# The last mantissa bits on GpSimd, and the product with v ahead of the sinks' transposes

## The chip, the cores and the metric

The program runs on one core of a Trainium2 chip. That core has five engines, each with an instruction queue of its own that is worked off in order: TensorE (PE in the profile, its weight loads PEld), VectorE (DVE), ScalarE (ACT), GpSimd (POOL) and SyncE (SP), which here only issues DMA transfers. The metric is the device time of one execution in microseconds (us), from repeated runs; one further execution is recorded by the profiler.

## The reference, cut to what matters

Attention over 2 batches, 8 heads, 768 positions and head size 64. A query sees the first 4 positions (the sinks) and a window of 128 positions behind it. A feed-forward layer (512 to 2048 and back) and a mixing layer over channels and positions follow.

```
keep = is_sink | in_window
scores = np.where(keep, scale * q @ k.T, -1e9)
a = softmax(scores);  x = a @ v
x = x + relu(layernorm(x) * g_ln @ w_ch1) @ w_ch2
theta = x @ w_theta
u = x + w_tok_r @ (x * cos(theta)) + w_tok_i @ (x * sin(theta))
out = u + relu(u @ w_ch)
```

## The kernel before, in words

**Pieces.** The 2 x 768 positions are cut into six pieces of 256 (two tiles of 128); pieces 0 to 2 are batch 0, pieces 3 to 5 batch 1. `attn_fast` walks the 48 steps (piece, head). In a step PE computes the scores of both tiles (L274 and L275, or L278), DVE adds the mask and takes the maximum (L381), and ACT the exponential (L384). One step later `turn_w` has PE transpose the window's weights into a PSUM bank (L397), and ACT and DVE copy them out as two 16-bit parts (L400, L401).

**Sinks.** The first tile of a batch sees the sinks inside its own window, so pieces 0 and 3 (those that begin a batch) have no sinks apart. The other four do: their weights for the first 16 positions are transposed on their own by `turn_sinks` (two transposes, L410) into columns 256 to 511 of a bank, from which ACT (L411) and DVE (L412) copy them into one of three `ws` buffers. That is 4 pieces x 8 heads = 32 times.

**The product with v.** One step after that, `values` multiplies the transposed weights with v (L426) into columns 0 to 127 of a bank called `pv`, and `normalize` (L441, DVE) scales the result into x. `finish` takes one `pv` bank for two things that belong to two different steps: the sinks' transposes of the step just turned, and the product with v of the step before it. The product reads the `ws` that was written one step earlier.

**Order.** PE's order is written out by hand: the generator of the attention yields between its parts, and `run` fills in the feed-forward layer's products (`first` L605 and L625, `second` L651) from the moment the first piece is normalised. With one piece in the feed-forward layer its products are half as wide as with two. The order on ACT, DVE, POOL and SP is set by the compiler's scheduler. Three to seven PSUM banks are handed round (`bank`).

**Weights.** They arrive as 64-bit floats. `load64` puts together a 32-bit float from one: DVE masks the sign and the top (L502), ACT scales the high word (L503), ACT takes the last mantissa bits from the low word (L505, a 16-bit read with step 4 and a 16-bit write with step 2), and DVE joins the parts (L506). It runs for 32 tiles of 128x512 (feed-forward weights, within the first 90 us) and 20 more later (theta 4, tok 12 of 128x768, ch 4). SP issues the loads (L498) into a few staging buffers, which L506 frees. Each weight is then split into two parts, by ACT (L593, L668) and POOL (L594, L669). POOL also splits q and k (L234, L249), scales and splits v (L204, L205) and adds up x in the gate (L722).

Of the kernel before, what the change touches and what calls it, by code (L numbers as in the profile page):

```python
# [14 lines left out]
AF = mybir.ActivationFunctionType  # L15
ALU = mybir.AluOpType
# [55 lines left out]
class Net:  # L72
# [207 lines left out]
    def attn_fast(self, eng):  # L280

        steps = [(piece, h) for piece in range(NP) for h in range(H)]
        nc, p, qk, pending, turned, late = self.nc, self.att, {}, [], [], []

        def load(j, eng=eng):
            if j < len(steps):
                piece, h = steps[j]
                if piece >= STACKED:
                    qk[piece, h] = self.stack_qk(piece, h, nc.gpsimd)
                elif h % 2 == 0:  # L290
                    qk[piece, h] = qk[piece, h + 1] = self.split_qk(piece, h // 2, eng)

        def load_v(piece):
            if piece < NP:
                b, tiles = self.tiles(piece)
                for t in tiles + ([NT] if tiles[-1] >= 2 else []):
                    self.split_v(b, t)

        def first_of_all(piece):
            return self.ahead() if piece == 0 else ExitStack()  # L300

        def turn():

            piece, h, pt, st = pending.pop(0)
            b, tiles = self.tiles(piece)
            with first_of_all(piece):
                wt, blocks = self.turn_w(pt, tiles)
            p["ws"].append(p["ws"].pop(0))
            turned.append((piece, h, wt, p["ws"][-1], blocks, st))
            return (pt, p["ws"][-1]) if tiles[0] else None  # L310

        def finish(sinks, ready):

            bank = self.bank("pv")
            if sinks:
                self.turn_sinks(bank, *sinks)
            if not ready:
                return
            piece, h, wt, ws, blocks, st = turned.pop(0)
            b, tiles = self.tiles(piece)  # L320
            with first_of_all(piece):
                self.values(bank, b, h, tiles, piece, wt, ws, blocks, st)
                if h % (H // 2) == H // 2 - 1:
                    self.stats(piece, h // (H // 2))
            if h == V_RANGE:
                while late:
                    q, ts = self.tiles(late.pop())
                    for t in ts:
                        with self.behind():
                            self.range_v(q, t)  # L330
            if h == H - 1:
                with first_of_all(piece):
                    self.norm(piece)
                late.append(piece)

        load(0, self.nc.vector)
        load_v(0)
        for j, (piece, h) in enumerate(steps + [(NP, 0)] * (TURN + LAG)):
            if j < len(steps):
                b, tiles = self.tiles(piece)  # L340
                if h == 0:
                    self.x[piece] = self.xp.tile([128, PIECE, DM], F32, tag=f"x{piece}", name=f"x{piece}")
                if piece < STACKED:
                    load(j + 2)
                if piece >= STACKED or h == H - 1 and piece + 1 == STACKED:
                    load(j + 1)
                if h == (3 if piece else V_NEXT):
                    load_v(piece + 1)
                pt, st = yield from self.softmax(h, tiles, qk[piece, h])
                pending.append((piece, h, pt, st))  # L350
            sinks = None
            if len(pending) > (TURN if j < len(steps) else 0):
                sinks = turn()
                yield
            ready = len(turned) > (LAG if j < len(steps) + TURN else 0)
            if sinks or ready:
                finish(sinks, ready)
                yield
        for t in tiles:
            self.range_v(b, t)  # L360
# [51 lines left out]
        nc.vector.scalar_tensor_tensor(out=ws[32:32 + NSK], in0=ps, scalar=PSC, in1=ws[0:NSK], op0=ALU.mult,  # L412
                                       op1=ALU.subtract)

    def values(self, pv, b, h, tiles, piece, wt, ws, blocks, st):

        nc = self.nc
        hc = slice(h * D, (h + 1) * D)
        for i in range(len(tiles)):
            prods = [(wt[:, x + e * len(blocks)], v[:, hc]) for e in range(2) for x, (j, t) in enumerate(blocks) if j == i  # L420
                     for v in self.v3[b, t][:2 - e]]
            if tiles[0]:
                vk = self.v3[b, NT]
                prods += [(ws[0:32 + NSK, i], vk[0:32 + NSK, 0, hc]), (ws[0:NSK, i], vk[0:NSK, 1, hc])]
            for j, (a, m) in enumerate(prods):
                nc.tensor.matmul(pv[:, i * D:(i + 1) * D], a, m, start=j == 0, stop=j == len(prods) - 1)  # L426
        self.normalize(h, pv, st, self.x[piece])

    def tiles(self, piece):
# [63 lines left out]
    def load64(self, src, stage, dst, tag):  # L493

        nc = self.nc
        n = dst.shape[-1]
        raw = stage.tile([128, n, 2], I32, tag=tag, name="raw")
        nc.sync.dma_start(out=raw.rearrange("p n w -> p (n w)"), in_=src.bitcast(I32))  # L498
        hi, flat = raw[:, :, 1], raw.rearrange("p n w -> p (n w)")
        half = flat.bitcast(U16).rearrange("p (n w) -> p n w", w=4)  # L500
        parts = dst.bitcast(U16).rearrange("p (n w) -> p n w", w=2)
        nc.vector.tensor_scalar(out=parts[:, :, 1], in0=half[:, :, 3], scalar1=0x8000, scalar2=None, op0=ALU.bitwise_and)  # L502
        nc.scalar.activation(hi.bitcast(F32), hi.bitcast(F32), AF.Copy, scale=2.0 ** -112)  # L503

        nc.scalar.activation(parts[:, :, 0], half[:, :, 1], AF.Copy, scale=2.0 ** -13, bias=2.0 ** -14 - 0.5)  # L505
        nc.vector.scalar_tensor_tensor(out=dst, in0=hi, scalar=3, in1=dst, op0=ALU.logical_shift_left,  # L506
                                       op1=ALU.bitwise_or)

# [537 lines left out]
```

## Time and profile before

| | |
|---|---|
| median of 3 runs | 755.43 us (754.74 to 755.86) |
| the profiled execution's own time | 753.02 us |
| its span | 751.2 us |
| PE busy | 650.8 us (87%) |
| DVE busy | 367.9 us (49%) |
| ACT busy | 365.6 us (49%) |
| POOL busy | 273.8 us (36%) |
| mean granted TensorE clock | 0.928 |

The span is the time from the first to the last instruction; 1.8 us of the profiled execution lie around it. Busy is the time in which an engine had at least one instruction running. [...]

### The profile page before, as it was taken

Reading aid. Unit: us, or ns where it says so; the run is one execution under the profiler, and the core shown is the slowest. Engines: PE = TensorE matmul, PEld = TensorE weight load, DVE = VectorE, ACT = ScalarE, POOL = GpSimd, SP = SyncE. Lnnn points to the kernel's source line nnn. Section 1 sums busy time; section 2 is a strip of 40 time slices with the busy share of each in tenths; the row PEclk is TensorE's granted clock in tenths of the full one; section 3 lists DMA queues with packets and bytes.
Section 4 is the critical chain, followed back from the end, with each engine's and each line's share of the span. In section 5 each row is a group of like instructions: output and inputs, shape, how many; then the busy total and the mean of one; then the engine's idle time right before and its main releaser. Section 6 shows DMA issues by size and latency. Waiting matters only on the chain.

```text
span 751.2 us, 10135 instructions
## 1 busy us (share of the span) xinstructions
PE 650.8 (87%) x3747; PEld 523.7 (70%) x3747; DVE 367.9 (49%) x808; ACT 365.6 (49%) x774; POOL 273.8 (36%) x240
## 2 busy tenths in 40 slices
PE   3845898789889997889888889999989989899996
PEld 2633556666667675666656667778878988899996
DVE  5889624432335434353333434321367878874442
ACT  5798724344445563444434425643456656552220
POOL 3143102422437585444354117654402343330000
PEclk9999758778999998989989969999999999999999
DMA  6587401100211131110110011310011232200102
GB/s 242 185 312 262 176 20 32 30 16 0 60 31 52 44 97 40 37 38 19 37 38 1 0 57 60 123 43 0 1 31 55 85 127 71 85 15 29 37 15 82
DMA packets 19339, 50.38 MB, mean 67 GB/s; under 512 B 2769, under 2 KB 5841, under 8 KB 19281
## 3 DMA queue, kind: packets, MB, share of 16 engines
q1 hardware_dynamic: 19280, 49.66, 19.8%
q8 instruction: 31, 0.51, 0.3%
q14 instruction: 28, 0.22, 0.1%
HBM read 46.50 MB, written 3.15 MB: 66 GB/s over the span
## 4 chain that ended last, share of the span: by engine, by line
PE 38%; DVE 6%; ACT 3%; issue 1%; POOL 1%; DMA 1%; ACTq 0%; POOLq 0%; DVEq 0%
PE m L736 11%; PE h L625 8%; PE acc L651 7%; PE f L767 4%; PE th L695 4%; PE pv L426 1%; DVE st L506 1%; DVE hl L630 1%; DVE st L502 1%; DMA raw<-wtok 1%; PE tp L680 1%; DVE k L705 1%; ACT hh L629 0%; PE s L275 0%; DMA raw<-wth 0%
## 5 line engine op out<-in xcount | busy, mean ns | idle before, releaser
L594 POOL TENSOR_TENSOR wl<-w,wh 128x512 fp32r<-128x512 f32 x92 | 119.6, 1304 | 176.2 <-ACT wh L593 105.4
L625 PE MATMUL h<-xT,wh 128*128 128x512 f32 (+1 forms) x408 | 115.1, 419 | 7.6 <-DVE hl L630 7.6
L593 ACT ACTIVATE wh<-w 128x512 fp32r<-128x512 f32 x102 | 63.9, 628 | 111.0 <-PE acc L651 66.3
L625 PEld LDWEIGHTS h<-xT,wh 128*128 128x128 f32 x408 | 75.0, 210 | 27.0 <-DVE hl L630 11.2
L426 PE MATMUL pv<-v,wt 128*128 128x64 f16 x528 | 33.3, 206 | 64.9 <-DVE ws L412 55.7
L381 DVE CUSTOM_DVE_ANT_0 p<-s,mask 128x272 f32<-128x272 f32 (+1 forms) x96 | 39.4, 414 | 99.4 <-PE s L275 59.5
L651 PE MATMUL acc<-wh,hh 128*128 128x512 f32 x182 | 80.2, 441 | 0.0
L426 PEld LDWEIGHTS <-wt 128*128 128x128 f16 x528 | 26.4, 105 | 76.9 <-issue 69.0
L651 PE MATMUL acc<-wh,hl 128*128 128x512 f32 x182 | 75.1, 412 | 0.0
L651 PE MATMUL acc<-wl,hh 128*128 128x512 f32 x182 | 74.3, 408 | 0.0
L384 ACT ACTIVATE p<-p,st 128x272 f32<-128x272 f32 (+1 forms) x96 | 47.4, 494 | 51.4 <-DVE st L381 51.2
L630 DVE SCALAR_TENSOR_TENSOR hl<-h,hh 128x512 fp32r<-128x512 f32 (+1 forms) x51 | 32.1, 630 | 63.7 <-ACT hh L629 63.7
L625 PE MATMUL h<-xT,wl 128*128 128x512 f32 (+1 forms) x204 | 54.8, 394 | 0.0
L625 PEld LDWEIGHTS h<-xT,wl 128*128 128x128 f32 x204 | 39.8, 208 | 7.9
L722 POOL TENSOR_TENSOR x<-xh,xl 128x512 f32<-128x512 f32 x12 | 19.0, 1582 | 72.0 <-DVE r L716 67.2
L401 DVE SCALAR_TENSOR_TENSOR wt<-wp,wt 128x512 f16<-128x512 f32 (+1 forms) x48 | 30.7, 641 | 24.1 <-ACT wt L400 24.0
L651 PEld LDWEIGHTS acc<-wh,hl 128*128 128x128 f32 x182 | 35.9, 197 | 8.4
L651 PEld LDWEIGHTS acc<-wh,hh 128*128 128x128 f32 x182 | 35.7, 196 | 8.4
L503 ACT ACTIVATE raw<-raw 128x512 f32<-128x512 f32 (+1 forms) x52 | 36.8, 720 | 8.7 <-DVE st L502 7.6
L651 PEld LDWEIGHTS acc<-wl,hh 128*128 128x128 f32 x182 | 36.1, 198 | 5.3
L234 POOL TENSOR_TENSOR lo<-raw,hi 128x672 fp32r<-128x672 f32 (+1 forms) x11 | 18.2, 1658 | 56.4 <-ACT hi L233 56.3
L397 PE MATMUL wp<-ident,p 128*128 128x128 f32 x176 | 34.8, 322 | 2.0 <-ACT p L384 1.1
(291 smaller groups left out, 1611.2 us busy)
## 6 DMA issues: line engine op xcount, KB each, us to landing
raw<-w SPq DMA_DIRECT2D x32, 512.0 KB, 5.0
raw<-wtok SPq DMA_DIRECT2D x12, 768.0 KB, 4.2
raw<-qk SPq DMA_DIRECT2D x32, 168.0 KB, 3.0
vr<-vt SPq DMA_DIRECT2D x14, 256.0 KB, 2.7
out_dram<-o SPq DMA_DIRECT2D x24, 128.0 KB, 1.7
raw<-qk SPq DMA_DIRECT2D x20, 136.0 KB, 2.7
raw<-qk SPq DMA_DIRECT2D x8, 336.0 KB, 3.4
raw<-wth SPq DMA_DIRECT2D x4, 512.0 KB, 3.2
```

The lines of the kernel that those rows point to most:

```text
L381: self.newest = [nc.vector.tensor_tensor_reduce(out=e, in0=ps[:, c0:WIN], in1=self.mask[min(t, 2)], scale=-0.125, scalar=3e38, op0=ALU.add ...
L384: nc.scalar.activation(e, e, AF.Exp, bias=st[:, 0, i:i + 1], scale=-1.0, accum_out=st[:, 1, i:i + 1])]
L397: nc.tensor.transpose(ps[:, x * 128:(x + 1) * 128], pt[:, i, c0:c0 + 128], self.ident)
L401: nc.vector.scalar_tensor_tensor(out=wt[:, m:2 * m], in0=ps, scalar=PSC, in1=wt[:, 0:m], op0=ALU.mult, op1=ALU.subtract)
L426: nc.tensor.matmul(pv[:, i * D:(i + 1) * D], a, m, start=j == 0, stop=j == len(prods) - 1)
L503: nc.scalar.activation(hi.bitcast(F32), hi.bitcast(F32), AF.Copy, scale=2.0 ** -112)
L593: nc.scalar.activation(hi, r, AF.Copy)
L594: (nc.vector if u >= UNITS - 5 else nc.gpsimd).tensor_tensor(out=lo, in0=r, in1=hi.bitcast(F32), op=ALU.subtract)
L625: nc.tensor.matmul(ps[:, 0:n], a[:, k * 128:(k + 1) * 128], x[:, k, c], start=m == 0, stop=m == 11)
L630: nc.vector.scalar_tensor_tensor(out=hl, in0=ps[:, 0:n], scalar=0.0, in1=hh.bitcast(F32), op0=ALU.max, op1=ALU.subtract)
L651: nc.tensor.matmul(ps, a[:, c], w, start=m == 0 and n == 0, stop=m == NF - 1 and n == len(prods) - 1)
L736: nc.tensor.matmul(ps, z[i][e][:, c * 128:(c + 1) * 128], w[:, t], start=s == 0 and m == 0 and c % 2 == 0, stop=s == NT - 1 and m == 5 and ...
```

## The change

In `finish`, the sinks' transposes are no longer issued first into the shared bank: `values` issues the product with v, then the transposes, then the normalisation. Where there is no product yet, the transposes are issued alone. In `load64`, line 505 becomes a GpSimd `tensor_scalar` of the same operands and constants in place of ScalarE's activation.

```diff
         def finish(sinks, ready):
             bank = self.bank("pv")
-            if sinks:
-                self.turn_sinks(bank, *sinks)
             if not ready:
-                return
+                return self.turn_sinks(bank, *sinks)
             piece, h, wt, ws, blocks, st = turned.pop(0)
             b, tiles = self.tiles(piece)
             with first_of_all(piece):
-                self.values(bank, b, h, tiles, piece, wt, ws, blocks, st)
+                self.values(bank, b, h, tiles, piece, wt, ws, blocks, st, sinks)
...
-    def values(self, pv, b, h, tiles, piece, wt, ws, blocks, st):
+    def values(self, pv, b, h, tiles, piece, wt, ws, blocks, st, sinks):
...
                 nc.tensor.matmul(pv[:, i * D:(i + 1) * D], a, m, start=j == 0, stop=j == len(prods) - 1)
+        if sinks:
+            self.turn_sinks(pv, *sinks)
         self.normalize(h, pv, st, self.x[piece])
...
-        nc.scalar.activation(parts[:, :, 0], half[:, :, 1], AF.Copy, scale=2.0 ** -13, bias=2.0 ** -14 - 0.5)
+        nc.gpsimd.tensor_scalar(out=parts[:, :, 0], in0=half[:, :, 1], scalar1=2.0 ** -13, scalar2=2.0 ** -14 - 0.5,
+                                op0=ALU.mult, op1=ALU.add)
```

## Rows read from the trace of the kernel before

**Rows 1.** Busy time by stretch: instructions in brackets, PEclk, DMA share, GB/s

```profile
85.00:225.00 140.00, 118.86 (x608) 84.98 (x606) 50.14 (x143) 56.34 (x144) 40.33 (x37) 0.80 0.09 26
225.00:285.00 60.00, 58.34 (x326) 43.76 (x326) 27.24 (x81) 35.44 (x90) 43.06 (x44) 1.00 0.21 61
285.00:446.00 161.00, 136.38 (x723) 98.72 (x722) 59.68 (x161) 65.72 (x160) 63.19 (x58) 0.89 0.10 28
```

**Rows 2.** PE's waits (us, times, longest): span, 0-85, 85-225, 225-285, 285-446

```profile
PE pv L426 <- DVE ws L412: 55.7, 32, 7.9
...
PE pv L426 <- DVE ws L412: 14.4, 3, 7.9
...
PE pv L426 <- DVE ws L412: 19.8, 14, 2.0
PE tp L571 <- DVE xn L554: 2.3, 1, 2.3
...
PE h L625 <- DVE hl L630: 1.1, 1, 1.1
...
PE pv L426 <- DVE ws L412: 22.5, 16, 2.5
```

**Rows 3.** Timeline 46 to 55 us (start, duration, idle before, releaser)

```profile
46.20 0.63 PE L410 MATMUL pv<-ident,p 128*16 128x128 f32 x2
50.05 0.36 ACT L411 ACTIVATE ws<-pv 16x256 f16<-16x256 f32 x1
54.27 0.41 DVE L412 SCALAR_TENSOR_TENSOR ws<-pv,ws 16x256 f16<-16x256 f32 x1
54.74 0.64 PE L426 MATMUL pv<-v,wt 128*128 128x64 f16 x9 [7.91 <-DVE ws L412]
```

**Rows 4.** Timeline 215 to 218 us, one step with sinks

```profile
215.39 0.38 PE L410 MATMUL pv<-ident,p 128*16 128x128 f32 x2
217.08 0.41 DVE L412 SCALAR_TENSOR_TENSOR ws<-pv,ws 16x256 f16<-16x256 f32 x1
217.55 0.34 PE L426 MATMUL pv<-v,wt 128*128 128x64 f16 x6 [1.78 <-DVE ws L412]
```

**Rows 5.** Stretches of 2 us around a gap, PE alone

```profile
166.00:168.00 2.00, 0.78 (x14) 1.00 0.01 4
168.00:170.00 2.00, 2.00 (x10) 0.63 0.04 8
170.00:172.00 2.00, 2.00 (x6) 0.50 0.00 0
```

**Rows 6.** Line 505 (ns: min/median/max; first and last start)

```profile
L505 ACT ACTIVATE w<-raw x32: 751/772/809, 14.9 to 87.2; 128x512 uint16<-128x512 uint16 x32
L505 ACT ACTIVATE st<-raw x20: 773/1080/1099, 445.0 to 661.3; 128x768 uint16<-128x768 uint16 x12, 128x512 uint16<-128x512 uint16 x8
```

**Rows 7.** Groups of POOL by form: busy us, mean ns, idle before

```profile
L594 POOL TENSOR_TENSOR wl<-w,wh 128x512 fp32r<-128x512 f32 x92 | 119.6, 1304 | 176.2 <-ACT wh L593 105.4 <-PE h L625 66.9 <-PE s L274 3.8
L204 POOL TENSOR_SCALAR vr<-vr 128x512 f32<-128x512 f32 x8 | 5.2, 644 | 16.0 <-DVE wt L401 12.8 <-DVE x L441 1.9 <-ACT st L435 0.7
```

**Rows 8.** Busy time of two stretches in which weights are made

```profile
6.93:69.00 62.07, 36.11 (x198) 28.04 (x198) 51.48 (x140) 52.24 (x127) 20.36 (x17) 1.00 0.72 258
585.00:645.00 60.00, 54.99 (x386) 51.35 (x385) 48.48 (x58) 36.97 (x55) 22.71 (x13) 0.97 0.28 94
```

**Rows 9.** Line 502 on DVE, then its timeline beside POOL at 48 us

```profile
L502 DVE TENSOR_SCALAR w<-raw x32: 435/459/1886, 13.5 to 87.6; 128x512 uint16<-128x512 uint16 x32
...
47.58 1.86 POOL L234 TENSOR_TENSOR lo<-raw,hi 128x672 fp32r<-128x672 f32 x1 [6.23 <-ACT hi L233]
47.88 2.23 DVE L502 TENSOR_SCALAR w<-raw 128x512 uint16<-128x512 uint16 x2
```

**Rows 10.** PE's longest wait after 600 us, and POOL's waits at L722

```profile
PE m L736 <- POOL tok31l L669: 2.1, 1, 2.1
...
POOL x L722 <- DVE r L716: 67.2, 11, 16.2
```

## What the change is expected to do

> **What bounds the kernel now.** I first cut the span by what PE does. From 446 us to the end PE is nearly always busy. From 85 to 446 us, where attention and the feed-forward layer are interleaved, three stretches differ [rows 1]. From 225 to 285 us PE is busy 58.34 of 60 us at a granted clock of 1.00. Before it PE is busy 118.86 of 140 us at 0.80, after it 136.38 of 161 us at 0.89. No other engine is near its limit in these two: ACT has 66 of 161 us, POOL 63.
>
> The waits of PE say what fills the gaps [rows 2]. One line dominates the run: the product with v (L426) waits for the sinks' copy on DVE (L412), 32 times, 55.7 us. By stretch that is 19.8 us and 22.5 us in the two disturbed ones and nothing in the middle, which holds piece 3, whose steps have no sinks. (The three stretches' rows sum to 33 waits and 56.7 us: one of 1.0 us is counted on both sides of 85 us.) So the undisturbed stretch is a sample, inside this run, of what PE does without the wait.
>
> The timeline shows the mechanism [rows 4]: PE ends the sinks' transposes at 215.8 us and stands until DVE has emptied them, 1.78 us. It is the bank and not the data that makes it wait. The first case [rows 3] proves it: the product at 54.74 us belongs to piece 0 (nine products in a row, none with `ws`; a step with sinks breaks off after six for those with `ws` [rows 4]), yet it waits 7.91 us for L412. Where a product does read `ws`, it is the one written a step earlier.
>
> The gaps also cost clock. [...] Lost in this way: 118.86 x 0.20 = 23.8 us and 136.38 x 0.11 = 15.0 us, 38.8 us together [rows 1].
>
> **The order in the bank.** After the change the product stands ahead of the transposes, so nothing of this step has to leave the bank before it. L410, L411, L412 and L441 all remain; L441 now queues on DVE behind L412, and only the statistics at the end of half a piece need it. On PE the work behind the product comes forward, and the bank is next wanted several products later. What is late next is what already shows in the sample: DVE's `hl` [rows 2]. The idle time now is 21.1 + 24.6 = 45.7 us [rows 1]. The sample's share, 1.66 of 60 us or 2.8%, over a new length of some 236 us leaves 6.6 us; the wait of 2.3 us for piece 1's normalised rows [rows 2] has another cause and stays. Gain: 45.7 - 6.6 - 2.3 = **36.8 us**.
>
> The clock should come back with the gaps, as in the sample. I take 60% before 225 us, since part of that stretch runs the feed-forward layer with one piece only and has no sample, and 85% after: 14.3 + 12.7 = **27.0 us**. Bounds: 0 and 38.8.
>
> **The start.** Two more waits lie there, 14.4 - 1.0 = 13.4 us [rows 2]. They are long because L411 and L412 queue behind weights: L410 ends at 46.8, L411 runs at 50.05, L412 at 54.27 us [rows 3]. ACT and DVE are both busy some 52 of 62 us there [rows 8], so PE freed from one wait will meet the next, for the window's weights or for the scores' copies. I take **4 us**, between a gain of 10 and a loss of 5 (next part).
>
> **The bits on POOL.** ACT loses 32 x 0.772 = 24.7 us in the first 90 us and 20 of 1.08 us or less from 445 us on [rows 6]. No row shows POOL doing this 16-bit strided operation. Nearest are its one-input `tensor_scalar` of as many elements, 0.644 us, and, far above, the two-input one at 1.304 us [rows 7]. I take 0.644, since engine, operation and size agree, and 1.5 times that for 768 columns: 20.6 us early, 12 x 0.97 + 8 x 0.644 = 16.8 us late; by the other end, twice that. POOL has room for it: it is busy 20.36 of 62 us and 22.71 of 60 us in the two stretches where weights are made [rows 8].
>
> Its place in the queues can cost. L505 waits on POOL for the weight's transfer, and behind it stand the splits of q, k and the weights (L234, L594, L669), which PE waits for. DVE's L506 now waits for POOL too, with the softmax's L381 and L401 behind it; the staging buffer comes free later, and SP's loads, those of q and k among them, queue behind that. On the other side L503 no longer shares ACT with L505. After 600 us PE waits for these weights already, 2.1 us for the longest [rows 10]. There I take a **loss of 2 us**, between a gain of 1 and a loss of 8.
>
> A row speaks against the move: of 32 L502 the median is 0.459 us but the longest 1.886 us, and two that run beside a POOL operation take 2.23 us [rows 9]. [...]
>
> [...]
>
> **Sum.** -36.8 - 27.0 - 4 + 2 = -65.8 us against the profiled execution's own 753.0 us: 687.2. That execution is 2.4 us below the median of the runs, so the forecast on the median's scale is 689.6, rounded to **690 us**.
>
> **The rivals.**
> 1. *The waits go, the clock stays low.* For it: PE also waits for other things, and one gap can cost many us of clock. Against it: the sample at 1.00. Time: 690 + 27 = 717.
> 2. *The wait moves on.* PE reaches the next product early and stands there for `wl`, `hl` or a bank, for half of each gap, and half of the clock's gain stays away: 690 + 18 + 14 = 722. Against it: in the sample POOL is busy 43 of 60 us [rows 1] and PE still waits 1.1 us only.
> 3. *DVE pays for POOL.* Each new POOL operation blocks a DVE one. DVE is busy 83% and 81% in the two weight stretches [rows 8]. The start loses 5 in place of gaining 4, and of the 16.8 us late some 12 reach PE: 690 + 9 + 10 = 709.
> 4. *Slower.* L722 waits on POOL for the gate's product (L716), 67.2 us in 11 cases, 6.1 us each [rows 10]. If the scheduler puts L505 behind it, the late weights are each late by that much: 690 - 2 + 67, and with 9 lost at the start 764. It decides once more than 66 / 20 = 3.3 us per late operation reach PE. Against it: L505's input is there long before L716's result.
> 5. *The change does not do what it says*: the product meets the same release at another place, and the time stays at 755. Against it: rows 3, where no data is in play.
>
> **How the numbers follow.** The forecast has 0.57, the rivals in order 0.14, 0.08, 0.11, 0.05 and 0.05. About 0.2% is what a measurement of this kernel can tell from no change. Faster: 0.57 + 0.14 + 0.08 + 0.11 = 0.90. The fifth is split, 0.04 within 0.2% and 0.01 above; with the fourth slower has 0.06. The range's low end takes the whole clock (12 more), the wait for piece 1 (2), 6 more at the start and no loss late: 690 - 22 = 668. The high end is the second rival with 4 of the DVE price: 726. Between them lie nearly all of the forecast and the first three rivals, about 8 in 10 with what is unknown of the scheduler's new order.
>
> **What would show it.** Right: L426 no longer waits for L412; from 85 us on the stretches with sinks run at 97% busy and a clock near 1.00; L505 shows about 0.65 us on POOL; the feed-forward layer starts a few us before 69 us. The clock's step is wrong if the gaps are gone and the clock is below 0.95; the wait's step if new lines stand in PE's waits with 15 us or more. The POOL step is wrong if L502 and L506 grow, or if PE's waits after 600 us for `tok` grow beyond some 10 us. What would upset the forecast most is a new order of ACT, DVE and POOL, which the scheduler makes afresh and which no row can show.

## The result, and the profile after

The changed kernel takes 679.14 us (median of 4, 676.54 to 680.67) against 755.09 us beside it (745.96 to 755.86): a ratio of 0.9016, 95% interval 0.8941 to 0.9090. The forecast was 690 us with a range of 668 to 726. One execution of a kernel below, `own_bank`, took 850.15 us at a mean granted clock (the share of TensorE's full speed, as the profile gives it) of 0.677; its ratio leaves this one out, its median counts it (680.2 us without).

Where the time went is read from three landmarks on PE: the first product of the feed-forward layer, the last product with v, and the end. First the rows of both lines in each trace, before above (L605, L426) and after below (L606, L424): instruction count, durations in ns (min/median/max), first and last start in us.

```profile
L605 PE MATMUL h<-x,w x40: 379/632/794, 69.1 to 115.5; 128*128 128x256 f32 x40
L426 PE MATMUL pv<-vk,ws x128: 197/199/233, 64.5 to 447.0; 48*128 48x64 f16 x64, 16*128 16x64 f16 x64
...
L606 PE MATMUL h<-x,w x40: 379/379/763, 68.0 to 100.5; 128*128 128x256 f32 x40
L424 PE MATMUL pv<-vk,ws x128: 197/199/231, 50.7 to 363.8; 48*128 48x64 f16 x64, 16*128 16x64 f16 x64
```

After, the last product with v starts at 363.8 us. So the start moved from 69.1 to 68.0 us (-1.1), the middle shrank from 377.9 to 295.8 us (-82.1), and what follows grew from 304.2 to 313.8 us (+9.6): -73.6 us in all, as the spans say (751.2 and 677.6). The busy times of the middle, counted from 85 us on, and of the rest, before above and after below, in the columns of [rows 1]:

```profile
85.00:447.00 362.00, 314.58 (x1665) 228.13 (x1662) 137.60 (x385) 157.93 (x392) 146.58 (x138) 0.87 0.11 33
447.00:751.20 304.20, 287.54 (x1853) 259.49 (x1852) 164.63 (x246) 139.18 (x223) 99.80 (x68) 0.98 0.16 55
...
85.00:363.80 278.80, 269.55 (x1647) 199.44 (x1646) 137.73 (x390) 157.00 (x390) 151.60 (x142) 0.99 0.16 46
363.80:677.60 313.80, 288.09 (x1853) 260.38 (x1852) 175.82 (x247) 124.43 (x205) 124.49 (x88) 0.98 0.16 54
```

In the middle PE is now busy 269.55 of 278.8 us at 0.99, where it was busy 314.58 of 362 us at 0.87. Later, PE does the same instructions (1853) in 288.09 in place of 287.54 us of busy time, but idles 25.7 in place of 16.7 us; DVE's busy time there has risen from 164.63 to 175.82 us.

PE's waits after (us, times, longest), to be held against [rows 2]:

```profile
PE tp L572 <- DVE xn L555: 17.1, 2, 11.9
PE h L626 <- DVE hl L631: 13.9, 8, 4.8
...
PE pv L424 <- DVE wt L399: 6.2, 3, 3.9
...
PE pv L424 <- DVE ws L410: 0.5, 1, 0.5
```

The 55.7 us for the sinks' copy have become 0.5 us. New at the top are two waits for normalised rows, of 11.9 us (piece 0, before the start) and 5.1 us (piece 1). The timeline of the first step with sinks answers [rows 3]:

```profile
45.30 0.69 PE L424 MATMUL pv<-v,wt 128*128 128x64 f16 x9
45.79 0.61 PE L408 MATMUL pv<-ident,p 128*16 128x128 f32 x2
...
50.20 0.41 DVE L410 SCALAR_TENSOR_TENSOR ws<-pv,ws 16x256 f16<-16x256 f32 x1
```

The nine products of piece 0 run at 45.3 us, 9.4 us earlier than before, while DVE empties the sinks at 50.2 us, when the product no longer stands behind it.

The groups of the weights' lines (busy us, mean ns, idle before), the first two rows of before and the rest of after (L506 became L507), with their mean ns:

```profile
L506 DVE SCALAR_TENSOR_TENSOR w<-raw,w 128x512 int32<-128x512 int32 x32 | 22.6, 717 | 2.8 <-ACT raw L503 2.6
L502 DVE TENSOR_SCALAR w<-raw 128x512 uint16<-128x512 uint16 x32 | 20.3, 658 | 4.9 <-DMA raw<-w 4.6
...
L507 DVE SCALAR_TENSOR_TENSOR w<-raw,w 128x512 int32<-128x512 int32 x32 | 29.7, 940 | 2.1 <-ACT raw L503 1.4 <-POOL w L505 0.6
L502 DVE TENSOR_SCALAR w<-raw 128x512 uint16<-128x512 uint16 x32 | 24.2, 778 | 0.0
...
L505 POOL TENSOR_SCALAR w<-raw 128x512 uint16<-128x512 uint16 x32 | 29.8, 931 | 9.0 <-DMA raw<-w 7.1
L505 POOL TENSOR_SCALAR st<-raw 128x768 uint16<-128x768 uint16 x12 | 16.4, 1369 | 1.1 <-DMA raw<-wtok 0.2
L505 POOL TENSOR_SCALAR st<-raw 128x512 uint16<-128x512 uint16 x8 | 7.7, 966 | 5.3 <-DMA raw<-wth 4.7
```

POOL takes 53.9 us for what was costed at 37.4, and DVE's two operations on each early tile have grown from 1.38 to 1.72 us.

### The profile page after: what moved, and what is told of

It reads as the page before. It is cut to its first block, busy times and chain, and to the rows that moved or that the text cites. A ratio compares the mean times of both kernels' runs of the same rounds, so it can differ in the third digit from the quotient of the medians.

```text
span 677.6 us, 10236 instructions
## 1 busy us (share of the span) xinstructions
PE 607.2 (90%) x3747; PEld 497.3 (73%) x3747; DVE 386.3 (57%) x808; ACT 331.5 (49%) x722; POOL 329.8 (49%) x292
## 4 chain that ended last, share of the span: by engine, by line
PE 62%; DVE 20%; ACT 6%; issue 5%; POOL 3%; DMA 3%; SPq 0%; DVEq 0%; POOLq 0%; ACTq 0%
PE h L626 17%; PE acc L652 17%; PE m L737 5%; PE pv L424 5%; PE f L768 5%; PE s L278 3%; PE wp L395 3%; PE s L275 2%; DVE st L507 2%; DVE zl L721 2%; DVE w L507 2%; DVE st L502 2%; ACT raw L503 2%; PE th L696 2%; DVE w L502 2%
## 5 line engine op out<-in xcount | busy, mean ns | idle before, releaser
L595 POOL TENSOR_TENSOR wl<-w,wh 128x512 fp32r<-128x512 f32 x92 | 120.3, 1310 | 118.8 <-ACT wh L594 79.3
L626 PE MATMUL h<-xT,wh 128*128 128x512 f32 (+1 forms) x408 | 104.6, 389 | 13.9 <-DVE hl L631 13.9
L626 PEld LDWEIGHTS h<-xT,wh 128*128 128x128 f32 x408 | 69.0, 193 | 30.4 <-DVE hl L631 17.1
L652 PE MATMUL acc<-wh,hh 128*128 128x512 f32 x182 | 77.6, 427 | 0.0
L652 PE MATMUL acc<-wh,hl 128*128 128x512 f32 x182 | 72.3, 397 | 0.0
L652 PE MATMUL acc<-wl,hh 128*128 128x512 f32 x182 | 72.0, 395 | 0.0
L382 ACT ACTIVATE p<-p,st 128x272 f32<-128x272 f32 (+1 forms) x96 | 47.4, 494 | 26.6 <-DVE st L379 26.4
L503 ACT ACTIVATE raw<-raw 128x512 f32<-128x512 f32 (+1 forms) x52 | 37.6, 731 | 44.4 <-DVE st L502 27.3
L723 POOL TENSOR_TENSOR x<-xh,xl 128x512 f32<-128x512 f32 x12 | 18.9, 1575 | 72.2 <-DVE r L717 72.1
L626 PE MATMUL h<-xT,wl 128*128 128x512 f32 (+1 forms) x204 | 50.6, 370 | 0.0
L424 PE MATMUL pv<-v,wt 128*128 128x64 f16 x528 | 32.3, 202 | 10.5 <-DVE wt L399 6.2
L626 PEld LDWEIGHTS h<-xT,wl 128*128 128x128 f32 x204 | 36.6, 192 | 6.7
L424 PEld LDWEIGHTS <-wt 128*128 128x128 f16 x528 | 24.2, 103 | 21.9 <-issue 9.9
L505 POOL TENSOR_SCALAR w<-raw 128x512 uint16<-128x512 uint16 x32 | 29.8, 931 | 9.0 <-DMA raw<-w 7.1
L395 PE MATMUL wp<-ident,p 128*128 128x128 f32 x176 | 32.6, 308 | 1.1 <-DVE vmax L216 0.8
```

The lines of the kernel that those rows point to most:

```text
L382: nc.scalar.activation(e, e, AF.Exp, bias=st[:, 0, i:i + 1], scale=-1.0, accum_out=st[:, 1, i:i + 1])]
L395: nc.tensor.transpose(ps[:, x * 128:(x + 1) * 128], pt[:, i, c0:c0 + 128], self.ident)
L595: (nc.vector if u >= UNITS - 5 else nc.gpsimd).tensor_tensor(out=lo, in0=r, in1=hi.bitcast(F32), op=ALU.subtract)
L626: nc.tensor.matmul(ps[:, 0:n], a[:, k * 128:(k + 1) * 128], x[:, k, c], start=m == 0, stop=m == 11)
L652: nc.tensor.matmul(ps, a[:, c], w, start=m == 0 and n == 0, stop=m == NF - 1 and n == len(prods) - 1)
```

## The experiments

The theory to test: the shared bank made PE stand, the gaps also lowered its clock, and the order alone undoes both; the bits on GpSimd gain nothing. The rivals: the relief of ScalarE has a part in it, or the clock was low for another reason. The table gives the kernels' times, and from each profile the start, the middle and the rest as read above.

| kernel | time, us | ratio to before (95%) | start | middle | rest |
|---|---|---|---|---|---|
| before (profile) | 755 | 1 | 69.1 | 377.9 | 304.2 |
| after | 679.1 | 0.902 (0.894 to 0.909) | 68.0 | 295.8 | 313.8 |
| order | 675.3 | 0.896 (0.892 to 0.900) | 70.6 | 297.7 | 310.1 |
| pool | 759.9 | 1.012 (1.007 to 1.016) | 68.2 | 370.5 | 309.2 |
| own_bank | 684.0 | 0.908 (0.901 to 0.916) | 64.8 | 306.1 | 307.5 |
| fill | 727.1 | 0.966 (0.962 to 0.971) | 70.2 | 350.6 | 304.3 |
| half | 710.8 | 0.940 (0.935 to 0.945) | 70.7 | 332.3 | 305.9 |
| act_act (as order) | 674.5 | 0.892 (0.889 to 0.896) | 69.0 | 297.2 | 310.0 |
| pool_early | 674.3 | 0.892 (0.889 to 0.896) | 67.5 | 296.9 | 308.1 |
| pool_late | 679.3 | 0.900 (0.896 to 0.903) | 69.4 | 293.7 | 314.4 |
| pool_pool (as after) | 679.3 | 0.899 (0.896 to 0.902) | 68.0 | 298.5 | 314.9 |
| spread | 669.2 | 0.885 (0.880 to 0.889) | 57.7 | 301.6 | 307.9 |
| ready | 667.8 | 0.882 (0.878 to 0.886) | 69.4 | 289.0 | 308.0 |
| both_steps | 672.2 | 0.888 (0.882 to 0.895) | 57.5 | 300.6 | 309.7 |

**Each part alone.** `order` is the changed kernel with line 505 back on ScalarE; `pool` is the kernel before with line 505 on GpSimd.

> The new order in the bank alone; the last mantissa bits stay on ScalarE. Theory: the middle of the run (first product of the feed-forward layer to the last product with v) gains its 83 us by the order alone, and the 9 us that the changed kernel loses after that belong to the bits on GpSimd: 665 to 673 us, and the feed-forward layer starts before 68 us because VectorE is no longer held up. Rival: the relief of ScalarE is part of the gain, and without it the middle gains some 65 us only: 690 to 700 us.

> The bits on GpSimd alone, in the old order. Theory: PE still waits some 55 us for the sinks' copy, and VectorE pays for GpSimd at the start and after 446 us: 757 to 770 us. Rival: ScalarE was what made the sinks' copy late, so that part of the waits goes with the bits too: 720 to 740 us.

The order alone takes 675.3 us and brings the whole gain of the middle (297.7 us); the rival's 690 to 700 did not come. The expectation missed in three points: the time lies 2 us above its 665 to 673, the start did not come forward (70.6 us), and the rest is 310.1 us, so not all of the 9.6 us there belong to the bits. The bits alone gain nothing: the median is 1.2% above before, and the executions of both overlap (749.81 to 764.20 us, and 749.59 to 759.20 beside them). PE waits 61.2 us for the sinks' copy in place of 55.7, so ScalarE's relief does not shorten those waits. (The profiled execution of `pool` was 10 us shorter than its median; its middle has a granted clock of 0.90 in place of 0.87. Its rest, at 0.98 as before, is 5.0 us longer.)

**Bank or data.** The old order, with a bank for each:

```diff
-            bank = self.bank("pv")
             if sinks:
-                self.turn_sinks(bank, *sinks)
+                self.turn_sinks(self.bank("sk"), *sinks)
             if not ready:
                 return
+            bank = self.bank("pv")
```

> The old order, but the sinks' transposes go into a bank of their own, allocated just before that of the product with v; the bits stay on ScalarE. Theory (PE waits for the bank, not for the data): the waits of the product with v for line 412 fall from 55.7 us to under 5, and the time to 665 to 690 us, as with the new order, less what the additional bank in the rotation costs. Rival (the product needs this step's sinks, or VectorE's queue is what is late for other reasons too): 740 to 756 us.

PE no longer waits for L412 before the product; what is left of that line is one wait of 2.1 us ahead of the transposes themselves:

```profile
PE h L625 <- DVE hl L630: 11.1, 9, 2.5
...
PE pv L426 <- DVE wt L401: 3.7, 4, 1.5
...
PE sk L410 <- DVE ws L412: 2.1, 1, 2.1
```

The sinks still go first here, on the same engines; only the bank differs. So the bank was the cause. The middle is 306.1 us, 8 more than in `order`, but it also begins 5.8 us earlier, so that the last product with v comes 2.6 us later. Five bank allocations per step in place of four may cost something; no run took that apart.

**What the gaps did to the clock.** The old order again, with work in the gap:

```diff
             if not ready:
                 return
+            if sinks:
+                fill = self.bank("fill")
+                lhs, rhs = turned[0][2], self.v3[self.tiles(turned[0][0])[0], self.tiles(turned[0][0])[1][0]][0]
+                for _ in range(6):
+                    nc.tensor.matmul(fill, lhs[:, 0], rhs, start=True, stop=True)
```

> The old order with six products of 512 columns (some 1.3 us at full clock) into a bank of their own between the sinks' transposes and the product with v, whose results nobody reads; so PE works where it stood. Theory (the gaps lower the clock): the time of the waits stays lost, but from 85 to 446 us the granted clock rises from 0.87 to over 0.96 and the run takes 715 to 735 us, though PE has 32 x 1.3 = 42 us more to do. Rival (the clock is low there for another reason): it stays at 0.87 to 0.90 and the time is 755 to 790 us.

The middle of this kernel, from 85 us to its last product with v, in the columns of [rows 1]:

```profile
85.00:420.80 335.80, 320.04 (x1851) 224.51 (x1850) 142.25 (x391) 161.36 (x403) 149.23 (x139) 0.98 0.13 37
```

PE does 186 more instructions there than before, and yet the middle, counted from the first product of the feed-forward layer, is 27.3 us shorter, since the granted clock is 0.98 in place of 0.87. The 192 products without a reader have 48.9 us of busy time, 1.53 us for six; the 1.3 expected is an estimate that fits the trace of before, where products of 512 columns start 0.23 us apart at a clock of 1.00 (L651 at 502 us). The gaps are mostly filled: in the stretch shown PE still waits for the sinks' copy 15 times, 7.4 us in place of 42.3. The time lost in them is still lost, as work that nobody needs. So low clock and gaps belong together, and the clock alone is worth at least those 27 us.

**Half of the heads.** Pieces 1 and 2 with the new order, pieces 4 and 5 with the old one, bits on ScalarE:

```diff
-            if not ready:
-                return self.turn_sinks(bank, *sinks)
+            if sinks and (turned[-1][0] >= 3 or not ready):
+                self.turn_sinks(bank, *sinks)
+                sinks = None
+            if not ready:
+                return
```

> The new order for pieces 1 and 2 only; for pieces 4 and 5 the sinks' transposes come first, as before; bits on ScalarE. Theory (each gap costs its own wait and the clock of the few us after it): the first stretch gains about what it lost, 19.8 us of waits and 23.8 us of clock, the second keeps 16 waits of some 22 us and a clock near 0.89; 705 to 718 us. Rival: the clock is set by the whole run's business, so that with half of the gaps gone it stays high in the second stretch as well: 690 to 700 us.

The two stretches with sinks, and PE's waits in the second one:

```profile
85.00:190.00 105.00, 99.86 (x643) 73.03 (x643) 54.19 (x153) 61.13 (x156) 43.63 (x40) 0.97 0.15 44
250.00:405.00 155.00, 131.08 (x721) 95.84 (x720) 58.99 (x157) 65.66 (x160) 62.26 (x58) 0.92 0.09 27
...
PE pv L427 <- DVE ws L413: 21.6, 15, 2.5
```

In one run the first stretch is clean (95% busy at 0.97) and the second nearly as it was (85% at 0.92; before, 85% at 0.89). At 710.8 us the kernel lies between the others: each stretch pays for its own gaps.

**Who takes the bits, early and late.** Four kernels with the new order; the bits of the 32 early and of the 20 late tiles on ScalarE or GpSimd:

```diff
-        nc.gpsimd.tensor_scalar(out=parts[:, :, 0], ...)
+        if tag != "raw":
+            nc.gpsimd.tensor_scalar(out=parts[:, :, 0], ...)
+        else:
+            nc.scalar.activation(parts[:, :, 0], half[:, :, 1], AF.Copy, scale=2.0 ** -13, bias=2.0 ** -14 - 0.5)
```

This is `pool_early`; `pool_late` has `tag == "raw"`.

> First of four kernels with the new order that differ only in who takes the last mantissa bits of the 32 early and of the 20 late weight tiles: here ScalarE both times (the order alone, timed beside the other three). Theory (the bits on GpSimd cost little, VectorE pays what ScalarE gains): 672 to 678 us, and the four lie within 8 us of each other. Rival (the bits bring a part of the gain): slowest of the four, by 5 us and more over the changed kernel.

> New order; GpSimd takes the bits of the 32 early tiles, ScalarE those of the 20 late ones. Theory: line 502 and the join grow at the start, since VectorE waits for GpSimd, and the first product of the feed-forward layer starts within 3 us of the 70.6 us that the order alone shows; 672 to 679 us. Rival: ScalarE's relief brings the start forward by 5 us and more.

> New order; ScalarE takes the bits of the 32 early tiles, GpSimd those of the 20 late ones. Theory: from the last product with v to the end the run loses 3 to 5 us against ScalarE both times (313.8 against 310.1 us in the two profiles), so 676 to 682 us. Rival: the late stretch differs by the new order alone and the bits there change nothing: within 1.5 us of ScalarE both times.

> The changed kernel itself beside the three others: GpSimd both times. Theory: 676 to 683 us, some 4 us above the order alone, by the late tiles. Rival: fastest of the four.

Timed side by side: 674.5 and 674.3 us with the late bits on ScalarE, 679.3 and 679.3 us with them on GpSimd. The early bits change nothing (`pool_early` starts at 67.5 us, 1.5 before `act_act`), the late ones cost 4.9 us. Here is the rest of the run, from the last product with v on, in the columns of [rows 1], first in `act_act` and then in `pool_late`:

```profile
366.20:676.20 310.00, 289.50 (x1853) 261.08 (x1852) 167.39 (x247) 140.31 (x225) 99.89 (x68) 0.97 0.16 55
363.10:677.50 314.40, 289.48 (x1853) 261.72 (x1852) 175.88 (x247) 124.47 (x205) 124.41 (x88) 0.98 0.16 54
```

PE is busy for the same time; DVE's same 247 instructions take 8.5 us longer, though only the engine of line 505 differs. PE's waits for `hl` in this stretch are 11.1 us (10.7 and 10.2 in the two profiles of the changed kernel) in place of 6.7 in `act_act` and `pool_early`. One such place, first in the changed kernel, then in `act_act`:

```profile
409.05 1.45 POOL L505 TENSOR_SCALAR st<-raw 128x768 uint16<-128x768 uint16 x1
410.58 1.26 POOL L595 TENSOR_TENSOR wl<-w,wh 128x512 fp32r<-128x512 f32 x1
410.64 2.02 DVE L507 SCALAR_TENSOR_TENSOR st<-raw,st 128x768 int32<-128x768 int32 x1 [1.04 <-ACT raw L503]
412.58 0.68 DVE L631 SCALAR_TENSOR_TENSOR hl<-h,hh 128x512 fp32r<-128x512 f32 x1
413.31 1.22 PE L626 MATMUL h<-xT,wh 128*128 128x512 f32 x2 [4.81 <-DVE hl L631]
...
410.58 0.96 DVE L506 SCALAR_TENSOR_TENSOR st<-raw,st 128x768 int32<-128x768 int32 x1 [1.23 <-ACT raw L503]
412.10 0.69 DVE L630 SCALAR_TENSOR_TENSOR hl<-h,hh 128x512 fp32r<-128x512 f32 x1 [0.56 <-ACT hh L629]
412.85 1.67 PE L625 MATMUL h<-xT,wh 128*128 128x512 f32 x4 [2.44 <-DVE hl L630]
```

With line 505 ahead of it on POOL, the weight's split (L595) slides over DVE's join; the join takes 2.02 us in place of 0.96, `hl` queues behind it though its input (`hh` on ACT) was ready at 411.0 us, and PE stands 4.81 in place of 2.44 us. Not all of that is the join's: PE got there 1.9 us earlier than in `act_act` and goes on 0.46 us later, and the join alone is 1.06 us longer.

**Two ways on.** `spread` issues the loads of weight tile 3 on behind the newest softmax; `ready` sets `READY1 = 5.5` in place of 6.5; `both_steps` does both. All have the new order and the bits on ScalarE.

```diff
             if u + AHEAD < NF:
-                self.load_w12(u + AHEAD)
+                with ExitStack() if general else self.behind():
+                    self.load_w12(u + AHEAD)
```

> The new order with bits on ScalarE, and the loads of weight tile 3 on are issued behind the newest softmax at their place in the program, so that the scheduler can't pull all 32 tiles into the first 90 us. Theory (at the start VectorE and ScalarE are held up by weights that nobody needs yet): the wait of 9 us for the first normalised rows shrinks and the feed-forward layer starts 5 us and more before the 69 us of the order alone; 662 to 671 us. Rival: the weights then come late or crowd the middle: 675 to 690 us.

> The new order with bits on ScalarE, and the attention of piece 1 is spread over 5.5 in place of 6.5 units of the feed-forward layer. Theory: PE's wait of 5.1 us for piece 1's normalised rows goes, since they are ready earlier: 668 to 673 us. Rival: PE waits for the attention of piece 1 instead, whose latency is packed tighter: 673 to 680 us.

> The new order with bits on ScalarE and both steps of before: weight loads held back, piece 1 spread over 5.5 units. Theory: the two gains lie in different places (the first rows of piece 0, the rows of piece 1) and add up: 669.2 - 674.5 + 667.8 = 662.5, so 660 to 666 us. Rival: held-back weights are what piece 1's tighter attention then collides with on VectorE: 667 us and more.

`spread` starts the feed-forward layer 11 us earlier, at 57.7 us, so it is the weights of the first 90 us that hold the start; some 4 us of it go again in the middle, which they now share (301.6 us). `ready` removes the wait for piece 1's rows; one wait of that kind is left:

```profile
PE tp L571 <- DVE xn L554: 9.2, 1, 9.2
```

At 667.8 us it is the fastest of all and beats both kernels of the study, 0.882 of before (0.878 to 0.886). The two do not add up: with both, a wait of 2.0 us for piece 1's rows is back, and `hl` costs 16.0 us in place of 11.1. The rival's time came (667 us and more), and `hl` is made on DVE, as the rival had it; no run took this collision apart.

## Why the prediction was right, and where it was off

**The sum.** The total came closer than its terms. On the scale of the spans 65.8 us were forecast and 73.6 came. The middle gave 82.1 us where 36.8 + 27.0 = 63.8 were forecast, 18.3 more; the start gave 2.9 less and the rest cost 7.6 more (9.6 in place of 2). These errors offset each other in part, and that is luck.

**The order.** Right in its mechanism and its size. Idle time of PE in the middle fell from 47.4 to 9.3 us (362 - 314.58 and 278.8 - 269.55), by 38.2 us; 36.8 was forecast. The wait for piece 1's rows, which the sum left at 2.3 us, became 5.1 us; PE now arrives earlier. With piece 0's 11.9 us the waits for rows are 17.1 us, above the 15 us that the prediction named as a sign against this step; but the 11.9 us lie before the start, where 13.4 us of the old waits stood.

**The clock.** The mechanism was right, the term was too small: this is the step that was mis-sized. 27.0 us was taken, 60% and 85% of what was lost. Lost before: 314.58 x 0.13 = 40.9 us; after: 269.55 x 0.01 = 2.7; given back 38.2 us, nearly the upper bound. Even this is too little, since the mean clock of a long stretch counts the gaps too, in which the clock can still be 1.00, as from 166 to 168 us; 0.63 and 0.50 follow there with PE busy throughout [rows 5]. Taken apart into stretches of 1 us, busy time x (1 - granted clock) sums to 44.8 us before and 2.3 us after: 42.5 us given back, above the bound of 38.8, which went by the mean. The reason given for the discount, that the first part has no sample, was no evidence for a lower clock there; the low clock followed the gaps in both parts. Of the 83.2 us by which the stretch from 85 us shrank (362 - 278.8), 2.5 us are then in neither term; PE also does 18 instructions fewer in it.

**The start.** 4 us was taken and 1.1 came. The two waits, 7.9 and 5.6 us, did go, and PE met a next wait, as the text said it would: 11.9 us for the first rows. In these 11.9 us DVE is busy throughout, 7.0 of them with weights (L502 and L507). `spread` shows what the start was held by.

**The bits on POOL.** The price was wrong: 0.644 us was taken from the row for 32-bit elements, and the operation takes 0.759 us at its shortest, 0.860 at the median and 0.931 on average. On the early tiles L502 grew from 0.658 to 0.778 us and L506 from 0.717 to 0.940 on average, which the prediction had named as the sign that this step is wrong. The loss late was put at 2 us between -1 and 8; between `act_act` and the two kernels with late bits on GpSimd it is 4.9 us. The third rival had this mechanism, DVE pays, at a higher price (12 us late, and 5 lost at the start). The join of 2.02 us is such a case: L595 runs on POOL from its start on, while in `act_act` the split comes only 0.63 us into the join, which takes 0.96. Why the join takes longer there was not shown. At the start DVE paid too: its two operations take 1.70 us a tile in `pool_early` and 1.44 in `act_act`, 8 us over the 32 tiles, yet the two kernels take the same time. What offset it was not taken apart.

**What stays open.** With the order alone the rest takes 310 us, 5.8 more than before, though nothing there was changed but what the scheduler made of it. (The profiled executions of `order` and `act_act` are 4.9 and 3.6 us above their medians; in `pool_early` and `ready`, profiled near their medians, it is 308 us.) PE waits 6.7 us for `hl` there in place of 4.7. In the part after the first theta product PE is busy 193.25 us at 0.97 in `act_act` and 190.47 at 0.99 before, for the same 1408 instructions, so 2.8 of these are a lower clock. Why waits and clock fell differently was not settled.

**The rivals.** The first, with the clock staying low, and the second, with half of the waits moving on, are excluded by the middle's 0.99 and 9.3 us. The fourth did not come: late L505 do stand behind the gate's sum (L722, now L723) in POOL's queue, but PE waits 2.2 us at most for a late weight, and the rest grew by 9.6 us and not by 67. The fifth is excluded by `own_bank` and the wait of 0.5 us.

## What to carry to other kernels

When an engine waits for data that it does not read, look for what the two share: here a PSUM bank used by two steps made one step's PE work wait for the other's evacuation, and the order in which PE fills it, or a second bank, decided it. A piece of the same run without the suspected wait is a good estimate of what its removal brings, clock included; the discount that was taken here without a row for it was the step that missed. Moving an operation off a busy engine can charge a third engine (here DVE, 1.38 to 1.72 us for its two operations on an early tile), so price it by what runs beside it, not by the operation alone.

## What the runs showed of the hardware that was not expected

The clock lost to gaps was as large as the gaps themselves: 40.9 us by the mean clock, 44.8 summed over stretches of 1 us, beside 42.3 us of waits in the same stretch. A gap filled with useless products (`fill`) made the kernel 3.4% faster. Executions of the kernel before differ by more than the 0.2% that the prediction took as what can be told: beside `ready` one took 746.80 us at a mean granted clock of 0.943 and another 756.80 at 0.928, while the four of `ready` took 666.98 to 668.77 at 0.983 to 0.987. In the middle of the profiled execution, from 85 to 447 us, the clock falls below 1.00 in 18 places, beside 30 waits for L412, so not each wait lowered it; whether that makes the difference between executions no run tested. And a `tensor_scalar` on GpSimd over 16-bit elements with step 4 takes 0.86 us (median, early tiles of the changed kernel) for 512 of them, where ScalarE takes 0.772 [rows 6].
